# Pooled attention and an MLP mixer on one core: another first batch, single tails for batches 1 and 2, and an ungated load

## The chip, the cores and the metric

The kernel runs on one core of one Trainium2 chip. The metric is the device time of one execution in microseconds (us). The time before is 296.34 us, the median of 3 runs (295.75 to 296.78). The traces come from the hardware profiler; times in them count from the start of the profiled span.

## The reference, cut to what matters

There are 8 batches with 8 heads, 576 tokens and a head size of 64. Keys and values are averaged over 8 tokens, then attention and a mixer with token and channel mixing follow.

```python
k_p = k.reshape(B, H, Sp, pool, D).mean(axis=3)      # Sp = 72, pool = 8
v_p = v.reshape(B, H, Sp, pool, D).mean(axis=3)
scores = scale * np.matmul(q, k_p.transpose(0, 1, 3, 2))
attn = softmax(scores)                               # over the 72 pooled tokens
x = np.matmul(attn, v_p)                             # heads side by side: (B, 576, 512)
h = np.maximum(x.transpose(0, 2, 1) @ w_tok1, 0.0) @ w_tok2    # 576 -> 256 -> 576
u = x + h.transpose(0, 2, 1)
out = u + np.maximum(u @ w_ch1, 0.0) @ w_ch2         # 512 -> 1536 -> 512
```

## The kernel before

**Tiles.** The 576 tokens of a batch are 512 main tokens, as 128 rows of 4 (index j), and a tail of 64 tokens. Tails of two batches share a tile of 128 rows: `groups = [[0, 7], [1, 2], [3, 4], [5, 6]]`, `group_of` gives a batch's group and `slot_of` its half of the rows (`half[0]` is rows 0 to 63, `half[1]` rows 64 to 127). Tiles that the text names: `km`, `qm`, `vm` hold a batch's main tokens in bf16 (two buffers each), `kt`, `qt`, `vt` the tails, `kbd` the pooled keys, `vpx` the pooled values with a column of ones, `qT` the transposed queries, `prob_m` and `prob_t` the exponentials, `pT` these transposed, `x_main` and `x_tail` the attention's output, `u_main` the token mixing's, `uT_main` that transposed, `GT` the hidden layer of the channel mixing. `pa` (six buffers of one bank) and `pt` (two) are the PSUM tiles.

**Steps of a batch.** `pool_k` and `pool_v` average keys and values by matmuls with a pooling matrix (`pool_m`, and `pool_t` for the tails, whose rows outside the batch's half are zero). A `Unit` is half of the main tokens and a `TailUnit` a tail tile; their steps are `do_qT` (transposes of q), `do_S` (scores, maximum and difference on VectorE), `do_E` (exp on ScalarE), `do_PT` (transposes of the exponentials) and `do_AV` (values, by the helper `values`: matmuls, then a reciprocal and a product on VectorE). Then `token_mix`: `do_AT` or `do_both_AT` (first layer), `do_u` (second layer and residual) and `do_uT` (transposes). For batches 0 and 1 the transposes of q and the exponentials are matmuls; from batch 2 on they are DMAs on SyncE's queue, and so are those of u from batch 1 on. `channel_mix` gives blocks of the first channel layer (`do_GT`, four matmuls of 512 columns) and thirds of the second (`do_out`). `keep_running` issues matmuls on a tile of zeros, whose results nobody uses.

**Order.** The order on the engines is written by hand. `first_stream` is batch 0 up to its transposed u. Then for each batch b the channel mixing of b (`c_stream`) is woven with a side stream: `second_stream` (batch 1's attention and token mixing) and `score_stream(2)` for b = 0, later `value_stream(b + 1)` and `score_stream(b + 2)`. `weave` takes from both in proportion to planned costs; `delay` is the planned cost of main work ahead of the first side step. Each engine executes its own instructions in this order, and waits in front of one whose data are not there.

**Loads.** All loads are issued on GpSimd's queue (software DMA), in this order: batch 0, the token weights, `w_ch1`, `load(1)`, `w_ch2`, `load(2)`. These stand in the program ahead of the streams. `load(b)` brings a batch's three main tiles; the tails of both batches of a group come with the first of them, except for group 0. `load(3)` and later are issued by `load_gated`: a small copy on GpSimd that reads a tile of the running stream, so that the loads behind it start only then. For batch 3 the gate is the first values of batch 1.

Of the kernel before, what the change touches and what calls it, by code (L numbers as in the profile page):

```python
# [48 lines left out]
def kernel(  # L49
# [60 lines left out]
    for t in tail_t[0]:  # L110
        nc.vector.memset(t[half[1]], 0.0)

    def load(b):
        g = group_of[b]
        if g and slot_of[b] == 0:
            tail_t[g] = [tail_pool.tile([P, H, D], BF16, name=n) for n in ("kt", "qt", "vt")]
        main_t[b] = [kv_pool.tile([P, H, NJ, D], BF16, name=n) for n in ("km", "qm", "vm")]
        for i in (0, 2, 1) if slot_of[b] else (0, 1, 2):
            src, mt, tt = (k, q, v)[i], main_t[b][i], tail_t[g][i]
            nc.gpsimd.dma_start(out=mt.rearrange("p h j d -> p h (j d)"),  # L120
                                in_=src[b, :, 0:MAIN, :].rearrange("h (p j) d -> p h (j d)", j=NJ))

            for bb in [b] if g == 0 else groups[g] if slot_of[b] == 0 else []:
                nc.gpsimd.dma_start(out=tt[half[slot_of[bb]]], in_=src[bb, :, MAIN:S, :].rearrange("h p d -> p h d"))
# [58 lines left out]
    x_tail[0] = singles.tile([P, DM], BF16, name="xt0")  # L183
    nc.any.memset(x_tail[0][half[1]], 0.0)
# [47 lines left out]
    def pool_k(b):  # L232
        g, s = group_of[b], slot_of[b]
        km, kt = main_t[b][0], tail_t[g][0]
        kp_ps = ps.tile([P, HP, SP], FP32, name="pa")
        if b == 0:
            keep_running(kp_ps.rearrange("p r n -> p (r n)"), 18)
        for pr in range(HP):
            for j in range(NJ):
                for hl in range(2):  # L240
                    nc.tensor.matmul(out=kp_ps[hl * D:(hl + 1) * D, pr, 0:SPM], lhsT=km[:, 2 * pr + hl, j, :],  # L241
                                     rhs=pool_m[:, 0:SPM], start=(j == 0), stop=(j == NJ - 1))
        for pr in range(HP):
            for hl in range(2):
                nc.tensor.matmul(out=kp_ps[hl * D:(hl + 1) * D, pr, SPM:SP], lhsT=kt[:, 2 * pr + hl, :],
                                 rhs=pool_t[s][:, SPM:SP], start=True, stop=True)
        heads = kbd[b % NB].rearrange("p (r t) e n -> p r t e n", t=2)
        for hl in range(2):
            src = kp_ps[hl * D:(hl + 1) * D]
            nc.scalar.copy(out=heads[0:D, :, hl, 0, :], in_=src)  # L250
            nc.vector.tensor_copy(out=heads[D:P, :, hl, 1, :], in_=src)  # L251
# [10 lines left out]
    class Unit:  # L262
# [40 lines left out]
        def do_PT(self, e):  # L303
            self.pT[e] = pt_pool.tile([P, H, P], BF16, name="pT")
            if not self.by_pe:
                nc.sync.dma_start_transpose(out=self.pT[e], in_=self.probs[:, e].rearrange("p h n -> p (h n)"))
                return
            pT_ps = ps_tr.tile([SP, H, P], BF16, name="pt")
            for h in range(H):
                nc.tensor.transpose(out=pT_ps[:, h, :], in_=self.probs[:, e, h, 0:SP], identity=ident)  # L310
            (nc.scalar.copy if self.first else nc.vector.tensor_copy)(out=self.pT[e][0:SP], in_=pT_ps)  # L311

        def do_AV(self, e):
            values(self.pT[e], x_main[self.b][:, 2 * self.jj + e, :], slice(0, P), [(slice(0, P), self.b)],
                   2 if self.first else 0)

    def values(pT, xo, rows, pieces, extra, place=lambda h: h):
        w = rows.stop - rows.start
        for hf in range(2):
            ao = ps.tile([P, HP, D + 1], FP32, name="pa")  # L320
            keep_running(ao.rearrange("p h d -> p (h d)"), extra)
            for hh in range(HP):
                h = hf * HP + hh
                for r, b in pieces:
                    nc.tensor.matmul(out=ao[r, hh, :], lhsT=pT[0:SP, place(h), r], rhs=vpx[b % NB][:, h, :],  # L325
                                     start=True, stop=True)

            den = sm_pool.tile([P, HP], FP32, name="den")
            nc.vector.reciprocal(out=den[rows], in_=ao[rows, :, D])  # L329
            nc.vector.tensor_tensor(  # L330
                out=xo[rows, hf * HP * D:(hf + 1) * HP * D].rearrange("p (h d) -> p h d", d=D),
                in0=ao[rows, :, 0:D], in1=den[rows, :, None].broadcast_to([w, HP, D]), op=ALU.mult)

    class TailUnit:
# [19 lines left out]
        def do_S(self):  # L354
            w = self.rows
            sc = [ps.tile([P, HP, SP], FP32, name="pa") for _ in range(2)]
            for pr in range(HP):
                for hl in range(2):
                    for b in self.bs:
                        r = half[slot_of[b]]  # L360
                        nc.tensor.matmul(out=sc[hl][r, pr, :], lhsT=self.qT[hl * D:(hl + 1) * D, pr, r],
                                         rhs=kbd[b % NB][hl * D:(hl + 1) * D, 2 * pr + hl, hl, :],
                                         start=True, stop=True)
            self.sh = []
            for hl in range(2):
                mx = sm_pool.tile([P, 8], FP32, name="mx")
                nc.vector.tensor_reduce(out=mx[w, 0:HP], in_=sc[hl][w], axis=AX.X, op=ALU.max)
                sh = sh_pool.tile([P, 6, SP], FP32, name="sh")
                nc.vector.tensor_tensor(out=sh[w, 0:HP], in0=sc[hl][w],
                                        in1=mx[w, 0:HP, None].broadcast_to([w.stop - w.start, HP, SP]),  # L370
# [3 lines left out]
        def do_E(self):  # L374
            w = self.rows
            self.probs = prob_t[self.g % 2]
            for hl in range(2):
                nc.scalar.activation(out=self.probs[w, hl, :, 0:SP], in_=self.sh[hl][w, 0:HP], func=AF.Exp, scale=scale)

        def do_PT(self):  # L380
            w = self.rows
            self.pT = pt_pool.tile([P, H, P], BF16, name="pT")
            if not self.by_pe:
                nc.sync.dma_start_transpose(out=self.pT, in_=self.probs.rearrange("p e h n -> p (e h n)"))
                return
            pT_ps = ps_tr.tile([SP, H, P], BF16, name="pt")
            for h in range(H):
                nc.tensor.transpose(out=pT_ps[:, self.place(h), w], in_=self.probs[w, h % 2, h // 2, 0:SP],
                                    identity=ident[w, w])
            copy = nc.scalar.copy if self.first else nc.vector.tensor_copy  # L390
            copy(out=self.pT[0:SP, :, w], in_=pT_ps[:, :, w])

        @staticmethod
        def place(h):
            return (h % 2) * HP + h // 2

        def do_AV(self):
            values(self.pT, x_tail[self.g], self.rows, [(half[slot_of[b]], b) for b in self.bs],
                   2 if self.first else 0, self.place)

    def token_mix(b):
# [24 lines left out]
        def do_both_AT():  # L426
            at_ps = [ps.tile([P, DM], FP32, name="pa") for _ in range(2)]
            for m in range(2):
                mains(m, at_ps[m])
            for m in range(2):  # L430
                tails(m, at_ps[m])
            for m in range(2):
                acts(m, at_ps[m])
# [45 lines left out]
    def units(b):  # L479
# [4 lines left out]
        if g == 0:  # L484
# [6 lines left out]
        return parts[b]  # L491

# [3 lines left out]
    def mix_stream(st, b, pooled=()):  # L496
# [9 lines left out]
        if b == 0:  # L506
            add(2160, do_both_AT)
        else:
            add(1080, do_AT, 0)
            add(1080, do_AT, 1)  # L510
            for bb in pooled:
                add(KP, pool_k, bb)
# [7 lines left out]
    def first_stream():  # L520
# [4 lines left out]
        a, c, t = units(b)  # L525
        add(KP, pool_k, b)
        add(QT, a.do_qT, 0, HP)
# [4 lines left out]
        add(QT, c.do_qT, HP, H, copy=nc.vector.tensor_copy)  # L532
# [3 lines left out]
        add(0, c.do_E, 0)  # L536
        add(VP, pool_v, b)
        add(0, a.do_E, 1)
        add(SC, c.do_S, 1)
        add(0, a.do_E, 2)  # L540
        add(PT, a.do_PT, 0)
        add(SC, c.do_S, 2)
        add(PT, a.do_PT, 1)
        add(0, c.do_E, 1)
        add(QT, t.do_qT)
        add(AV, a.do_AV, 0)
        add(0, c.do_E, 2)
        add(SC, t.do_S)
        add(AV, a.do_AV, 1)
        add(PT, c.do_PT, 0)  # L550
        add(PT, c.do_PT, 1)
        add(AV, c.do_AV, 0)
        add(0, t.do_E)
        add(PT, t.do_PT)
        add(AV, c.do_AV, 1)
        add(AV, t.do_AV)
        mix_stream(st, b)
        return st

    def second_stream(st):  # L560
# [4 lines left out]
        add(KP, pool_k, b)  # L565
# [15 lines left out]
        add(0, load_gated, 3, lambda: x_main[1][:, 0, 0:1])  # L581
# [4 lines left out]
        add(KP, pool_k, 2)  # L586
        add(QT, t.do_qT)
        add(PT, c.do_PT, 0)
        add(2 * SC, t.do_S)
# [5 lines left out]
        add(VP, pool_v, 2)  # L595
        add(AV, t.do_AV)
        units(2)
        add(0, qT_dma, 2)
        mix_stream(st, b)

    def owned(b):

        g, s = group_of[b], slot_of[b]
        return [b] if g == 0 else groups[g] if s == 0 and g > 1 else []
# [56 lines left out]
    def channel_mix(uTs, us, dst, width):  # L661
# [37 lines left out]
        return [(864, do_GT(m0)) for m0 in range(0, NM, per)], out_pieces  # L699

    def c_stream(b):
# [11 lines left out]
        wide, chunk = channel_mix(uT_main[b], lambda j: u_main[b][:, j, :], dst_main, MAIN)  # L713
# [15 lines left out]
    load(2)  # L729
    engines = {mybir.EngineType.PE, mybir.EngineType.Activation, mybir.EngineType.DVE,  # L730
               mybir.EngineType.SP, mybir.EngineType.Pool}
    with tc.manual_schedule(engines=engines):
        weave(Stream(), first_stream())
        for b in range(B):
# [8 lines left out]
            weave(c_stream(b), side, 0.0 if b == 0 else 3456.0 if b == 1 else 1728.0, 3456.0 if b == B - 2 else 1728.0)  # L743
# [30 lines left out]
```

## Time and profile before

| | us |
|---|---|
| median of 3 runs | 296.34 |
| lowest, highest | 295.75, 296.78 |
| the profiled execution's own time | 295.11 |
| its span, first to last instruction | 293.4 |
| TensorE busy | 278.4 |
| VectorE, ScalarE, GpSimd busy | 166.3, 122.5, 49.3 |

The lines of the profile are read as follows. Engines are PE (matmul), PEld (weight load), DVE (VectorE), ACT (ScalarE), POOL (GpSimd) and SP (SyncE). A line of the timeline has the start and the length in us, the engine, the line of the kernel, the operation, output and inputs, and in brackets the idle time of the engine before it with what ended it. In the table of stages, a number in brackets is a count of instructions.

### The profile page before, as it was taken

How to read it: one execution, taken by the hardware profiler on the slowest of the kernel's cores; microseconds unless marked ns; L12 is line 12 of the kernel's file. 1: busy time of each engine (PE TensorE's matmuls, PEld its weight loads, DVE VectorE, ACT ScalarE, POOL GpSimd, SP SyncE). 2: the span in 40 equal slices, each digit the busy share in tenths (PEclk: the TensorE clock that was granted, in tenths of full speed). 3: DMA queues.
4: the chain of work that ended last, by engine and by line, in shares of the span. 5: the costliest groups of instructions: out<-in, count | busy, mean ns of one | idle time of the engine just before them, and what ended most of it. 6: DMA issues, size and time to landing. Idle time of an engine off the chain costs nothing.

```text
span 293.4 us, 5564 instructions
## 1 busy us (share of the span) xinstructions
PE 278.4 (95%) x2234; PEld 148.8 (51%) x2234; DVE 166.3 (57%) x382; ACT 122.5 (42%) x225; POOL 49.3 (17%) x80
## 2 busy tenths in 40 slices
PE   6778999998999999999999999999999999999994
PEld 3554555544545545456545444465445444464463
DVE  4776478868638944385558653684559642530012
ACT  7473667203652445125543445035433552026320
POOL 8656606300120008000300032000000000000000
PEclk9799999999999999999999999999999999999999
DMA  7999999996999999959998999759425920341013
GB/s 86 187 204 196 188 205 198 187 207 115 218 168 150 174 230 155 192 121 161 171 186 141 181 185 175 117 160 169 103 53 123 167 73 36 92 108 36 36 38 108
DMA packets 106843, 42.54 MB, mean 145 GB/s; under 512 B 73921, under 2 KB 102209, under 8 KB 106817
## 3 DMA queue, kind: packets, MB, share of 16 engines
q0 software_dynamic: 41392, 17.93, 49.2%
q1 hardware_dynamic: 65280, 24.13, 41.3%
q8 instruction: 17, 0.28, 0.4%
q10 hardware_dynamic: 144, 0.13, 0.1%
q14 instruction: 10, 0.07, 0.1%
HBM read 35.85 MB, written 9.44 MB: 154 GB/s over the span
## 4 chain that ended last, share of the span: by engine, by line
PE 81%; DMA 6%; ACT 5%; DVE 5%; POOL 2%; issue 1%; DVEq 0%; POOLq 0%
PE pa L673 30%; PE pa L688 28%; PE pa L414 4%; PE pa L442 4%; PE pa L325 3%; DMA vm<-in_v_dram 3%; PE pa L258 2%; DMA qT<-qm 2%; PE pa L286 2%; ACT pT L311 1%; DMA uTm<-um 1%; PE pa L450 1%; DVE mx L289 1%; PE pa L241 1%; DVE sh L291 1%; PE pa L418 1%
## 5 line engine op out<-in xcount | busy, mean ns | idle before, releaser
L688 PE MATMUL pa<-wc,GT 128*128 128x512 bf16 (+1 forms) x444 | 104.4, 373 | 0.0
L673 PE MATMUL pa<-uTm,wc 128*128 128x512 bf16 x384 | 92.9, 379 | 1.3 <-DMA uTm<-um 1.3
L675 ACT ACTIVATE GT<-pa 128x512 bf16<-128x512 f32 x108 | 64.5, 597 | 69.6 <-PE pa L673 69.5
L673 PEld LDWEIGHTS <-wc 128*128 128x128 bf16 x576 | 45.8, 98 | 38.4 <-DVE mx L289 1.7
L688 PEld LDWEIGHTS <-GT 128*128 128x128 bf16 x444 | 41.6, 98 | 40.5
L299 ACT ACTIVATE prob_m<-sh 128x432 bf16<-128x432 f32 (+1 forms) x48 | 24.4, 521 | 53.6 <-DVE sh L291 34.0
L692 DVE TENSOR_TENSOR o<-pa,um 128x512 f32<-128x512 f32 (+1 forms) x33 | 22.2, 672 | 31.0 <-PE pa L688 30.9
L289 DVE TENSOR_REDUCE mx<-pa 128x6 f32<-128x432 f32 (+1 forms) x48 | 26.4, 550 | 4.6 <-PE pa L286 4.5
L291 DVE TENSOR_TENSOR sh<-pa,mx 128x432 f32<-128x432 f32 (+1 forms) x48 | 26.8, 558 | 3.7
L330 DVE TENSOR_TENSOR xm<-pa,den 128x256 bf16<-128x256 f32 x64 | 27.2, 425 | 2.3
L329 DVE RECIPROCAL den<-pa 128x4 f32<-128x4 f32 (+1 forms) x74 | 13.0, 176 | 22.8 <-PE pa L325 22.8
L447 DVE TENSOR_TENSOR um<-pa,xm 128x512 bf16<-128x512 f32 x30 | 20.1, 687 | 5.5 <-PE pa L442 5.4
L325 PEld LDWEIGHTS <-pT 72*128 72x128 bf16 (+1 forms) x320 | 14.4, 100 | 9.3 <-issue 2.1
L442 PE MATMUL pa<-AT,w2m 128*128 128x512 bf16 x64 | 18.1, 379 | 0.5 <-ACT AT L408 0.5
L410 DVE TENSOR_SCALAR AT<-pa 128x512 bf16<-128x512 f32 x8 | 5.5, 692 | 22.2 <-PE pa L418 22.2
L658 POOL COPY gate<-pT 128x1 bf16<-128x1 bf16 x4 | 0.8, 188 | 102.6 <-DMA pT<-prob_m 102.6
L286 PE MATMUL pa<-kbd,qT 128*128 128x144 bf16 x128 | 16.3, 234 | 1.0 <-DMA qT<-qm 0.5
L325 PE MATMUL pa<-vpx,pT 72*128 72x65 bf16 (+1 forms) x320 | 16.6, 194 | 0.4 <-ACT pT L311 0.4
L286 PEld LDWEIGHTS <-qT 128*128 128x128 bf16 x128 | 11.2, 101 | 10.8 <-ACT qT L277 1.2
L414 PE MATMUL pa<-xm,w1m 128*128 128x512 bf16 x64 | 16.3, 379 | 0.0
L251 DVE CAST kbd<-pa 64x288 bf16<-64x288 f32 x16 | 7.3, 456 | 12.1 <-ACT kbd L250 12.0
L230 PE MATMUL pa<-idle 128*128 128x288 bf16 (+2 forms) x44 | 10.8, 366 | 2.2 <-DVE pool_t L159 2.2
(99 smaller groups left out, 211.5 us busy)
## 6 DMA issues: line engine op xcount, KB each, us to landing
out_dram<-o SPq DMA_DIRECT2D x31, 256.0 KB, 2.5
km<-in_k_dram POOLq DMA_DIRECT2D x8, 512.0 KB, 7.8
vm<-in_v_dram POOLq DMA_DIRECT2D x8, 512.0 KB, 10.6
qm<-in_q_dram POOLq DMA_DIRECT2D x7, 512.0 KB, 10.0
wc<-in_moe_w_ch_dram POOLq DMA_DIRECT2D x6, 512.0 KB, 10.7
out_dram<-o SPq DMA_DIRECT2D x9, 128.0 KB, 2.4
kt<-in_k_dram POOLq DMA_DIRECT2D x8, 64.0 KB, 6.5
qm<-in_q_dram POOLq DMA_DIRECT2D x2, 256.0 KB, 5.1
```

Of the source, the lines that this page charges most:

```text
L286: nc.tensor.matmul(out=sc[:, (h - h0) * 2:(h - h0) * 2 + 2, :], lhsT=qTs[self.b][:, 2 * h + self.jj, :], rhs=kbd[self.b % NB][:, h], start ...
L289: nc.vector.tensor_reduce(out=mx[:, 0:n], in_=sc, axis=AX.X, op=ALU.max)
L291: nc.vector.tensor_tensor(out=sh[:, 0:n], in0=sc, in1=mx[:, 0:n, None].broadcast_to([P, n, SP]), op=ALU.subtract)
L299: nc.scalar.activation(out=self.probs[:, :, h0:h1, 0:SP].rearrange("p e h n -> p h e n"), in_=self.sh[i][:, 0:(h1 - h0) * 2].rearrange("p ...
L325: nc.tensor.matmul(out=ao[r, hh, :], lhsT=pT[0:SP, place(h), r], rhs=vpx[b % NB][:, h, :], start=True, stop=True)
L330: nc.vector.tensor_tensor(out=xo[rows, hf * HP * D:(hf + 1) * HP * D].rearrange("p (h d) -> p h d", d=D), in0=ao[rows, :, 0:D], in1=den[ro ...
L414: nc.tensor.matmul(out=at_ps, lhsT=w1m[:, j, m * P:(m + 1) * P], rhs=x_main[b][:, j, :], start=(j == 0), stop=False)
L442: nc.tensor.matmul(out=u_ps, lhsT=w2m[:, m, j, :], rhs=ATs[b][:, m, :], start=(m == 0 and not by_act), stop=(m == 1))
L673: nc.tensor.matmul(out=g_ps[:, i, :], lhsT=wc1[:, kk, m * P:(m + 1) * P], rhs=uTs[:, kk, :], start=(kk == 0), stop=(kk == 3))
L675: nc.scalar.activation(out=GT[:, m0:m0 + per, :], in_=g_ps, func=AF.Relu)
L688: nc.tensor.matmul(out=hold["ps"], lhsT=GT[:, kk, j * P:(j + 1) * P], rhs=wc2[:, kk, cols], start=(kk == 0), stop=(kk == NM - 1))
L692: nc.vector.tensor_tensor(out=o_sb, in0=hold["ps"], in1=us(j)[:, cols], op=ALU.add)
```

## The change

- Batch 0: the pooled keys of even and odd heads go to two PSUM banks, ScalarE copies the one and VectorE the other. Idle matmuls: 28 instead of 18 ahead of `pool_k`, 6 of 512 columns behind it (`warm`), and one instead of two for each half in `values`, where sums and values of all 8 heads now have one bank each and one reciprocal and one product. The tail's steps come earlier, the first token layer (`do_both_AT`) is in three pieces among the last values, and `pool_k` of batch 1 stands among the transposes of batch 0's u, its copies behind them.
- The first three blocks of batch 0's channel mixing are done in halves of 256 tokens (`do_early`), and its side stream starts behind a planned cost of 3456 instead of 0.
- A `TailUnit` of a single batch puts even and odd heads on the two halves of the rows of one bank, so that it has one maximum, one difference and one exp, and four transposes instead of eight. The tails of batches 1 and 2 are units of their own now: batch 1's is transposed by matmuls, batch 2's by DMAs. They still share the tiles `kt1`, `qt1`, `vt1`, which are no longer part of a pool; each batch loads its own half, and their other half is cleared first.
- `pool_k(2)` and `pool_v(2)` leave the second stream for batch 1's token mixing and batch 2's score stream.
- `load(3)` is called ahead of the streams, with no gate.

The diff, cut to its core:

```diff
+    tail_t[1] = [singles.tile([P, H, D], BF16, name=n) for n in ("kt1", "qt1", "vt1")]
     def load(b):
-        if g and slot_of[b] == 0:
+        if g > 1 and slot_of[b] == 0:
             tail_t[g] = [tail_pool.tile([P, H, D], BF16, name=n) for n in ("kt", "qt", "vt")]
...
-            for bb in [b] if g == 0 else groups[g] if slot_of[b] == 0 else []:
+            for bb in [b] if g < 2 else groups[g] if slot_of[b] == 0 else []:
                 nc.gpsimd.dma_start(out=tt[half[slot_of[bb]]], in_=src[bb, :, MAIN:S, :].rearrange("h p d -> p h d"))
...
+    for t in tail_t[1]:
+        nc.any.memset(t[half[1]], 0.0)
...
     def pool_k(b):
+        pool_k_copy(b, pool_k_sum(b))
+
+    def pool_k_sum(b):
         km, kt = main_t[b][0], tail_t[g][0]
-        kp_ps = ps.tile([P, HP, SP], FP32, name="pa")
+        kp_ps = [ps.tile([P, HP, SP], FP32, name="pa") for _ in range(2)]
         if b == 0:
-            keep_running(kp_ps.rearrange("p r n -> p (r n)"), 18)
+            keep_running(kp_ps[0].rearrange("p r n -> p (r n)"), 28)
...
-                nc.tensor.matmul(out=kp_ps[hl * D:(hl + 1) * D, pr, SPM:SP], lhsT=kt[:, 2 * pr + hl, :],
+                nc.tensor.matmul(out=kp_ps[hl][hl * D:(hl + 1) * D, pr, SPM:SP], lhsT=kt[:, 2 * pr + hl, :],
                                  rhs=pool_t[s][:, SPM:SP], start=True, stop=True)
+        return kp_ps
+
+    def pool_k_copy(b, kp_ps):
         for hl in range(2):
-            src = kp_ps[hl * D:(hl + 1) * D]
-            nc.scalar.copy(out=heads[0:D, :, hl, 0, :], in_=src)
-            nc.vector.tensor_copy(out=heads[D:P, :, hl, 1, :], in_=src)
+            src = kp_ps[hl][hl * D:(hl + 1) * D]
+            copy = nc.vector.tensor_copy if hl else nc.scalar.copy
+            copy(out=heads[0:D, :, hl, 0, :], in_=src)
+            copy(out=heads[D:P, :, hl, 1, :], in_=src)
...
     class TailUnit:
         def do_S(self):
-            sc = [ps.tile([P, HP, SP], FP32, name="pa") for _ in range(2)]
+            sc = [ps.tile([P, HP, SP], FP32, name="pa") for _ in range(len(self.bs))]
...
+                        dst = sc[hl][r, pr, :] if len(sc) > 1 else sc[0][half[hl], pr, :]
...
     def first_stream():
         add(KP, pool_k, b)
+        add(0, warm, 6)
...
-        mix_stream(st, b)
+        add(1080, do_both_AT, (0, 1), False, False)
         add(AV, c.do_AV, 0)
         add(AV, c.do_AV, 1)
+        add(1080, do_both_AT, (2,), True, False)
+        add(540, do_both_AT, (3,), False, True)
+        for j in range(NJ):
+            add(690, do_u, j)
+        add(224, do_uT, 0)
+        add(224, do_uT, 1)
+        k1 = []
+        add(KP, lambda: k1.append(pool_k_sum(1)))
+        add(224, do_uT, 2)
+        add(224, do_uT, 3)
+        add(0, lambda: pool_k_copy(1, k1[0]))
...
     def second_stream(st):
-        add(KP, pool_k, b)
...
-        add(0, load_gated, 3, lambda: x_main[1][:, 0, 0:1])
...
-        add(KP, pool_k, 2)
...
-        add(2 * SC, t.do_S)
+        add(SC, t.do_S)
...
-        add(VP, pool_v, 2)
-        add(AV, t.do_AV)
         units(2)
         add(0, qT_dma, 2)
-        mix_stream(st, b)
+        add(AV, t.do_AV)
+        mix_stream(st, b, owned(2))
...
     load(2)
+    load(3)
...
-            weave(c_stream(b), side, 0.0 if b == 0 else 3456.0 if b == 1 else 1728.0, 3456.0 if b == B - 2 else 1728.0)
+            weave(c_stream(b), side, 3456.0 if b <= 1 else 1728.0, 3456.0 if b == B - 2 else 1728.0)
```

## The prediction

> **Bounds now.** I read the busy times first, then the busy time of each engine by stage, then the timeline around the stages that the change touches, then GpSimd's own queue of loads with the time from issue to landing.
>
> ```profile
> PE 278.4 (95%) x2234; PEld 148.8 (51%) x2234; DVE 166.3 (57%) x382; ACT 122.5 (42%) x225; POOL 49.3 (17%) x80
> ```
>
> TensorE is busy for 278.4 of 293.4 us. Where the other 15 us lie is told by the stages (columns: stretch, its length, busy PE, PEld, DVE, ACT, POOL, granted clock, DMA, GB/s):
>
> ```profile
> 30.00:35.00 5.00, 4.50 (x74) 2.85 (x74) 2.19 (x5) 3.02 (x6) 3.59 (x5) 1.00 1.75 183
> 65.00:70.00 5.00, 4.49 (x33) 2.44 (x32) 4.12 (x8) 1.46 (x3) 0.00 (x0) 1.00 0.83 137
> 100.00:150.00 50.00, 50.00 (x384) 26.22 (x383) 28.01 (x68) 21.63 (x39) 9.76 (x14) 1.00 1.08 172
> 200.00:250.00 50.00, 50.00 (x347) 24.64 (x346) 27.20 (x67) 21.26 (x39) 0.00 (x0) 1.00 0.48 100
> ```
>
> From 100 to 250 us TensorE has no gap at all. So there is no slack to the right in which a late start could be caught up: what delays TensorE in the first 80 us delays the end by as much, and what it is given there is given to the end.
>
> Three places of the timeline fix the pace of that first part:
>
> ```profile
> 32.96 0.69 PE L241 MATMUL pa<-pool_m,km 128*64 128x64 bf16 x32
> 33.71 1.02 PE L673 MATMUL pa<-uTm,wc 128*128 128x512 bf16 x4
> 65.91 0.55 PE L286 MATMUL pa<-kbd,qT 128*128 128x144 bf16 x6 [0.51 <-DMA qT<-qm]
> 72.67 3.61 PE L673 MATMUL pa<-uTm,wc 128*128 128x512 bf16 x16 [1.27 <-DMA uTm<-um]
> ```
>
> At 32.96 the keys of batch 1 are pooled, at 33.71 the channel mixing of batch 0 begins, at 72.67 that of batch 1. The brackets are the only waits for a DMA between them: 0.51 and 1.27 us.
>
> The loads are a queue of their own:
>
> ```profile
> 20.10 0.88 POOL L120 DMA_DIRECT2D km<-in_k_dram  x1
> 20.98 1.38 POOL L124 DMA_DIRECT2D kt<-in_k_dram  x2
> 33.24 0.90 POOL L120 DMA_DIRECT2D km<-in_k_dram  x1
> 46.50 0.19 POOL L658 COPY gate<-xm 128x1 bf16<-128x1 bf16 x1 [9.57 <-DVE xm L330]
> 46.99 0.88 POOL L120 DMA_DIRECT2D km<-in_k_dram  x1 [0.30 <-PE pa L325]
> ```
>
> They land strictly in the order of issue, one behind the other. By the times to landing of single issues, batch 1's k lands at 20.10 + 8.7 = 28.8, its first k tail at 20.98 + 8.2 = 29.2, its last v tail at 29.05 + 7.6 = 36.6, the three pieces of w_ch2 at 29.72 + 9.5 = 39.2, 30.47 + 11.2 = 41.7 and 32.51 + 11.7 = 44.2. Batch 2's k, issued at 33.24, lands last of these:
>
> ```profile
> L120 POOL DMA_DIRECT2D km<-in_k_dram x1: 903/903/903, 33.2 to 33.2; - x1
> DMA to landing us min/median/max: 13.9/13.9/13.9
> ```
>
> So at 47.1 us. A 512 KB load takes 2.5 to 2.9 us of this queue and a tail 0.4 us, and it has no gap from the first landing on.
>
> **The wait.** The change adds one wait that decides the result. Before, the tails of batches 1 and 2 are both loaded by load(1), in one tile of 128 rows, and both halves are there at 29.6 when pool_k(1) runs at 32.96. After, load(1) brings rows 0 to 63 alone, and load(2) brings rows 64 to 127 of the same tile, kt1. But pool_k(1) still takes `kt[:, 2 * pr + hl, :]`, all 128 rows (the rows of the other batch meet zeros in pool_t). load(2) stands ahead of all streams in the program, so the tail matmuls of pool_k(1) must wait for a DMA of batch 2. The order of the changed program with its waits agrees: the first tail weight load of pool_k(1) waits for two DMA semaphores, one of batch 1's k tail and one that counts up to batch 2's k tail. That DMA now stands behind k, q and v of batch 1, all of w_ch2 and batch 2's k.
>
> When does it land? Between the landing of batch 1's k (28.8) and of batch 2's k (47.1) the queue loses three tails, 3 x 0.43 = 1.3 us, and batch 2's k tail adds 0.4: 47.1 - 1.3 + 0.4 = 46.2 us. GpSimd issues about eight loads ahead, as before, so the queue stays fed.
>
> Queued on TensorE behind the waiting weight load: the last two transposes of u of batch 0, the channel mixing of batch 0 and all that follows. ScalarE and VectorE wait for these in their turn. After 46.2 come the 8 tail matmuls (0.12) and the two transposes (2 x 0.22): the first block of channel mixing starts at 46.2 + 0.1 + 0.12 + 0.45 = 46.9. Before: 33.71. That is a delay of 13.2 us.
>
> **Its cover.** All edits of the first batch end before this wait. Two banks for the pooled k and one engine for each make four copies in a row (8.11 to 9.91, 1.8 us) two pairs side by side (0.9). Ten more idle matmuls end near 7.9 instead of 6.7, past k's landing at 7.2 (+0.6), and six of 512 columns cost 1.3 ahead of the q transposes. The tail halves its passes on VectorE (four of 0.45 become two), its two exps of 0.39 become one of some 0.43, one pT copy (0.96) leaves ScalarE, and of the first token mixing's ten matmuls (2.15 us, 25.98 to 28.1) only two follow the last values. Walking that order by these rows, TensorE comes to the waiting weight load near 30 to 31 instead of 33.5. All this is costed at nothing, because the wait ends at 46.2 whether TensorE came at 30 or at 36. Without that cover it would be worth about 3 us, as the first rival has it. The early half-width blocks of channel mixing are the same columns in pieces, 24 x 0.11 for 12 x 0.22, nothing. The ungated load(3) is worth nothing: before, its gate opened at 46.50 while load(2) filled the queue until 52.4, so the queue never ran dry. Now its q and v wait for batch 1's transposes and pool_v (52 to 55) and land by some 62; batch 3's scores come 30 us later.
>
> **The clock.** TensorE will stand still for some 15 us. What the trace shows of this:
>
> ```profile
> 2.17 4.50 PE L230 MATMUL pa<-idle 128*128 128x288 bf16 x18 [2.17 <-DVE pool_t L159]
> 11.00:12.00 1.00, 1.00 (x12) 1.00 (x10) 0.96 (x3) 0.17 (x1) 0.56 (x1) 0.50 1.39 184
> 12.00:13.00 1.00, 1.00 (x9) 0.60 (x7) 0.97 (x2) 0.87 (x2) 0.00 (x0) 0.50 1.71 177
> ```
>
> After the idle start, 18 matmuls took 0.24 us each, twice the pace of later ones, for 4.3 us. Between 5 and 10 us TensorE was busy for 3.3 of 5, and the granted clock then was 0.5 for 3.4 us (0.58, 0.50, 0.50, 0.71 in four stretches of 1 us). So after the long wait I expect half speed for 3.4 to 4.3 us, which loses half of that, 1.7 to 2.15. I take 1.9. Bounds: nothing if the clock were kept, 3.4 if half speed lasted twice as long. The Trainium skill (TensorE: Matmul & The Clock Gate, "What's actually happening") says that the clock falls to half after an idle window of about 3.4 us and comes back after one busy window of that length, wherever that window happens to begin. An estimate by that page alone would be 1.7 us, and the sum 0.2 us lower.
>
> **Next stage.** From there to the channel mixing of batch 1 it took 72.67 - 33.71 = 39.0 us before. The waits of 0.51 and 1.27 us for DMA transposes go, since the loads are done by 62 and these transposes come after 70: -1.8. The tail of batch 1 now has nothing between its transposes and its values. Before, pool_v(2) (1.1 us) and a block of 0.86 stood there, while VectorE worked off four value pairs and then copied pT, until 56.6, with the transposes done at 55.6. That is a new wait of 1.0. Two tails of 8 score and 8 value matmuls (0.32 and 0.26 each) instead of one of 16 (0.32 and 0.38) add 0.4, less 4 transposes that move to the DMA queue (0.2). Sum -1.8 + 1.0 + 0.2 = -0.6, between -1.8 (the new wait hidden) and +1.2 (the old ones stay). pool_k(2) moves behind batch 1's first token mixing, its k there since 46: nothing. Later stages keep their order; batch 7's tail loses two VectorE passes in a stage bound by TensorE: nothing.
>
> **Sum.** 13.2 + 1.9 - 0.6 = +14.5 us. The profiled execution took 295.11 us (span 293.4): 309.6. The median of the runs is 296.34, 1.2 above it: 310.8 us.
>
> **Rivals.** (1) Faster: the wait for batch 2's k tail does not hold TensorE, the two halves being kept apart. Then the first batch's gain of 3 us comes through up to 58 us, but there the scores of batch 2 wait for its q transposes, which landed at 65.9 before, 1.8 us after the last load (55.31 + 8.8 = 64.1). They may be issued near 52 now, yet the loads still end at 63 to 64, and a transposing DMA issued at 150.7 under loads landed 6.1 us later, where the median is 2.5. The end gains between 0 and 3, say 2: 294.3. It decides the other way if the tail matmuls start by 34. For it: the rows that pool_k(1) uses are there at 29.2. Against: it reads the whole tile, and the wait is in the order. Chance 0.03. The Trainium skill (DMA: Bandwidth & Descriptors, "Queues, rings and completion order") says that each DMA engine takes its queues in turn, packet by packet; by that these transposes would land under the loads, and this rival would keep the full 3 us, 293.3. (2) The clock stays full, or the wait is all that happens: 310.8 - 1.9 = 308.9. Against it stand the two stretches at half speed. Chance 0.10. (3) Half speed lasts twice as long and the new tail wait does not replace the old ones: +1.5 and +1.8, 314.1. Chance 0.05.
>
> **Numbers.** The forecast has 0.82. A measurement of this kernel tells about 0.3% (0.9 us) from no change; only the first rival comes near or below it. Faster 0.03, same 0.01, slower 0.96. The range takes in rival (2) less 0.9 us for the landing and the stage, and the forecast plus 2.2 us for a longer half-speed stretch: 308.0 to 313.0.
>
> **Signs.** Right: one TensorE gap of 15 to 16 us, ended by a DMA into kt at 45.5 to 47; granted clock 0.5 right behind it for 3 to 5 us; the first block of channel mixing at 46.5 to 48; batch 1's at 86 to 88; no gap from 100 to 250 us. Wrong: pool_k(1) goes through before 34 us, or the gap ends at another transfer, or TensorE comes back at full clock.

## The result and the profile after

The changed kernel takes 309.84 us, the median of 4 runs (309.58 to 310.35), for 296.04 us of the kernel before (the three runs above and a fourth, 294.78 to 296.78). The ratio is 1.0473, with a 95% interval of 1.0433 to 1.0513: slower. The forecast was 310.8 us. Below, each ratio is to runs of the kernel before that were made beside the run in question; their medians lie between 295.33 and 295.64 us. One run of all (301.08 us, in experiment 6) lies more than 1.5% above the fastest of its kernel and is left out of its ratio. The profiled execution took 309.79 us with a span of 308.1; before it was 295.11 with 293.4.

First the busy times of the profile's page:

```profile
PE 280.5 (91%) x2279; PEld 151.6 (49%) x2279; DVE 163.5 (53%) x372; ACT 123.5 (40%) x227; POOL 49.1 (16%) x79
```

TensorE has 2.1 us more of busy time than before, and some 12.6 us more of idle time. One gap alone is longer than that. The timeline of the changed kernel (start us, us, engine, line, operation, out<-in, count, and in brackets the idle time before it and what ended it):

```profile
30.00 0.69 PE L248 MATMUL pa<-pool_m,km 128*64 128x64 bf16 x32
46.24 0.38 PE L252 MATMUL pa<-pool_t,kt 128*64 128x8 bf16 x8 [15.55 <-DMA kt<-in_k_dram]
46.55 1.03 PE L502 MATMUL pt<-ident,um 128*128 128x128 bf16 x8
47.38 4.03 PE L756 MATMUL pa<-uTm,wc 128*128 128x256 bf16 x24
```

L248 is the main part of pool_k(1), L252 its tail part. The tail comes 15.55 us behind the main part, released by a transfer into kt, and the first block of channel mixing (L756) stands at 47.38, where it was 33.71. The issue of that transfer, and who waited for it:

```profile
L125 POOL DMA_DIRECT2D kt<-in_k_dram x1: 687/687/687, 32.5 to 32.5; - x1
...
  PEld L252: 15.7, 1
  PE pa L252: 15.5, 1
...
DMA to landing us min/median/max: 13.7/13.7/13.7
```

32.48 + 13.72 = 46.20: it is load(2)'s k tail, and its only customer is the tail of pool_k(1). The stages, with the same columns as before:

```profile
35.00:40.00 5.00, 0.00 (x0) 0.00 (x0) 0.00 (x0) 0.00 (x0) 2.26 (x3) 0.50 1.25 206
47.00:48.00 1.00, 1.00 (x9) 0.83 (x7) 0.77 (x2) 0.38 (x1) 0.42 (x1) 0.50 1.77 183
49.00:50.00 1.00, 1.00 (x7) 0.69 (x6) 0.00 (x0) 0.00 (x0) 0.88 (x2) 0.54 1.48 196
50.00:51.00 1.00, 1.00 (x11) 0.90 (x10) 0.00 (x0) 0.43 (x1) 0.48 (x1) 1.00 1.78 180
100.00:150.00 50.00, 49.69 (x410) 26.29 (x405) 33.13 (x70) 18.30 (x35) 6.94 (x10) 1.00 1.05 168
```

In the gap the granted clock falls to 0.50, and it comes back only at 49.9 us, 3.7 us after the matmuls start again. From 100 us on TensorE has no gap to speak of, as before.

Batch 1's channel mixing begins at 87.27 (72.67 before), 14.6 us later, and the span ends 14.7 us later. So the whole loss is made before 88 us and nothing of it comes back.

### The profile page after: what moved, and what is told of

Same layout as the page of the kernel before. It is cut to its first block, busy times and chain, and to the rows that moved or that the text cites. A ratio compares the mean times of both kernels' runs of the same rounds, so it can differ in the third digit from the quotient of the medians.

```text
span 308.1 us, 5672 instructions
## 1 busy us (share of the span) xinstructions
PE 280.5 (91%) x2279; PEld 151.6 (49%) x2279; DVE 163.5 (53%) x372; ACT 123.5 (40%) x227; POOL 49.1 (16%) x79
## 4 chain that ended last, share of the span: by engine, by line
PE 77%; DMA 12%; DVE 4%; POOL 4%; ACT 1%; issue 1%; DVEq 0%; POOLq 0%
PE pa L725 30%; PE pa L740 27%; DMA kt<-in_k_dram 4%; PE pa L444 4%; PE pa L482 3%; DMA qm<-in_q_dram 3%; DMA w2r<-in_moe_w_tok_dram 3%; PE pa L358 3%; PE pa L269 2%; PE pa L297 2%; DMA uTm<-um 1%; PE pa L756 1%; PE pa L248 1%; PE pa L448 1%; PE pa L490 1%; DVE um L487 1%
## 5 line engine op out<-in xcount | busy, mean ns | idle before, releaser
L727 ACT ACTIVATE GT<-pa 128x512 bf16<-128x512 f32 x105 | 62.6, 597 | 68.3 <-PE pa L725 68.2
L725 PE MATMUL pa<-uTm,wc 128*128 128x512 bf16 x372 | 89.8, 379 | 0.0
L725 PEld LDWEIGHTS <-wc 128*128 128x128 bf16 x564 | 45.0, 98 | 35.8 <-issue 0.2
L363 DVE TENSOR_TENSOR xm<-pa,den 128x256 bf16<-128x256 f32 x56 | 23.8, 425 | 1.9
L362 DVE RECIPROCAL den<-pa 128x4 f32<-128x4 f32 (+1 forms) x66 | 11.7, 177 | 21.9 <-PE pa L358 21.9
L358 PEld LDWEIGHTS <-pT 72*128 72x128 bf16 (+1 forms) x280 | 12.5, 100 | 8.9 <-issue 1.7
L252 PE MATMUL pa<-pool_t,kt 128*64 128x8 bf16 x64 | 2.3, 176 | 15.5 <-DMA kt<-in_k_dram 15.5
L358 PE MATMUL pa<-vpx,pT 72*128 72x65 bf16 (+1 forms) x280 | 14.1, 194 | 1.1 <-DVE pT L422 1.0
L444 PE MATMUL pa<-xm,w1m 128*128 128x512 bf16 x56 | 14.4, 379 | 0.0
```

What stands on the lines that cost most here:

```text
L358: nc.tensor.matmul(out=ao[r, hh, :], lhsT=probs_of(h, r), rhs=vpx[b % NB][:, h, :], start=True, stop=True)
L363: nc.vector.tensor_tensor(out=xo[rows, hf * HP * D:(hf + 1) * HP * D].rearrange("p (h d) -> p h d", d=D), in0=ao[rows, :, 0:D], in1=den[ro ...
L444: nc.tensor.matmul(out=at_ps, lhsT=w1m[:, j, m * P:(m + 1) * P], rhs=x_main[b][:, j, :], start=(j == 0), stop=False)
L725: nc.tensor.matmul(out=g_ps[:, i, :], lhsT=wc1[:, kk, m * P:(m + 1) * P], rhs=uTs[:, kk, :], start=(kk == 0), stop=(kk == 3))
L727: nc.scalar.activation(out=GT[:, m0:m0 + per, :], in_=g_ps, func=AF.Relu)
```

## Experiments

The theory: one shared tile makes batch 1's pooled keys wait for batch 2's k tail; the landing of that tail sets the time. Rivals: other edits of the change make the delay; the clock's loss is not real; and, once the wait is gone, something else holds the same time. What was expected is quoted as it was put down before each run.

### 1. Read only the batch's own rows

```diff
-lhsT=kt[:, 2 * pr + hl, :],  rhs=pool_t[s][:, SPM:SP]
+lhsT=kt[half[s], 2 * pr + hl, :],  rhs=pool_t[s][half[s], SPM:SP]
-lhsT=pool_t[s], rhs=vt
+lhsT=pool_t[s][half[s]], rhs=vt[half[s]]
```

> The changed kernel, except that the tail matmuls of pool_k and pool_v read only the 64 rows of their own batch (64 partitions of kt1 and pool_t for 128). Loads, order and everything else stay. Theory (one shared tile makes batch 1's pooled keys wait for batch 2's k tail): TensorE passes this place at 30.2 us, as the k tail of batch 1 landed at 29.3; the first block of channel mixing starts near 31 (46.9 was the forecast, 33.71 the kernel before); the whole delay goes and the first batch's gain of 2.8 us comes through: 292 to 294 us, the likeliest 293. Rival A (the delay is mainly from other edits: first batch's order, single tails, ungated fourth batch's loads): the time stays above 296. Rival B (the wait is only moved: the next shared tile, or the transposes of batch 2's q under the loads, holds TensorE instead): a wait of several us between 35 and 65, and 297 to 309.

Measured: 296.63 us (10 runs, 296.05 to 298.03), ratio to before 1.0046 (1.0024 to 1.0067). Its timeline:

```profile
30.26 0.69 PE L248 MATMUL pa<-pool_m,km 128*64 128x64 bf16 x32
30.88 0.29 PE L252 MATMUL pa<-pool_t,kt 64*64 64x8 bf16 x8
...
63.91 0.55 PE L297 MATMUL pa<-kbd,qT 128*128 128x144 bf16 x6 [1.37 <-DMA qT<-qm]
```

The tail follows the main part at once. With the same loads in the same order, 13.2 of the 13.8 us are gone: the wait makes them, and rival A falls as their cause, though 296.63 lies above the 296 that it named. The forecast of 293 was missed by 3.6 us. Rival B has a part in that: TensorE waits 1.37 us for batch 2's transposed q, and batch 1's channel mixing starts at 72.54, hardly earlier than before (72.67). Another 1.7 us are lost behind it, where no such wait shows (span 295.0 for 293.4). Experiments 5 to 9 take these apart.

### 2. The kernel before with one part of the change

```diff
-for bb in [b] if g == 0 else groups[g] if slot_of[b] == 0 else []:
+for bb in [b] if g < 2 else groups[g] if slot_of[b] == 0 else []:
```

> The kernel before, with one part of the change alone: load(1) brings only batch 1's tails, load(2) batch 2's, in the same shared tiles. First batch's order, the double tail and the gated fourth batch stay as before. Theory: its pool_k(1) waits for batch 2's k tail, which lands at 46.2; the first block of channel mixing starts at 46.4 for 33.71, +12.7; half speed behind it costs another 1.8; the waits of 0.5 and 1.3 us for transposes may go: 307.8 to 309.6 us. Rival A (other edits make the delay): within 1 us of 295 to 296.

Measured: 309.35 us (one run, span 307.6).

```profile
45.87 0.38 PE L245 MATMUL pa<-pool_t,kt 128*64 128x8 bf16 x8 [11.20 <-DMA kt<-in_k_dram]
```

One line of the load is enough to make the whole loss. TensorE came to it some 4 us later than in the changed kernel, so the gap is 11.20 for 15.55 us, and the time is the same within 0.5 us: this is the cover that the prediction claimed for the first batch's edits. The two are not alike term by term: here the first block stands at 46.18 for 47.38, and half speed lasts until 51.5 for 49.9.

### 3. A dose: the same tails earlier in the queue

```diff
 # in load_w_ch2, behind the first of its three pieces:
+if i == 0:
+    for src, tt in ((k, tail_t[1][0]), (v, tail_t[1][2])):
+        nc.gpsimd.dma_start(out=tt[half[1]], in_=src[2, :, MAIN:S, :]...)
 # and load(2) leaves these two out
```

> The changed kernel, with batch 2's k and v tails moved ahead in the queue of loads, behind the first third of w_ch2 and no longer behind batch 2's k and v. Reads of all 128 rows stay. Theory: batch 2's k tail lands 7.8 us earlier (38.4 for 46.2, behind one third of w_ch2 at 38.0); the wait of TensorE ends there and shrinks from 15.5 to 7.8 us; the time falls by the same 7.8 us to 302.0; half speed behind it, as the stand is still longer than 3.4 us, costs 1.8 as before. If the clock's loss went with the length of the stand, 301.1. Rival A: no change, 309.8.

Measured: 301.98 us (one run, span 300.3).

```profile
38.19 0.38 PE L255 MATMUL pa<-pool_t,kt 128*64 128x8 bf16 x8 [7.03 <-DMA kt<-in_k_dram]
```

The wait ends 8.05 us earlier and the time is 7.9 us lower. The landing sets the time one for one, and a stand of 7 us costs the clock about as much as one of 15: the stage rows of this run show half speed until 42.3, 4.2 us behind the stand, for 3.7 in the changed kernel. The variant in which the loss goes with the length of the stand (301.1) is out by 0.9.

### 4. TensorE kept busy while it waits

```diff
+if b == 1:
+    keep_running(ps.tile([P, DM], FP32, name="pa"), 68)   # ahead of the tail matmuls
```

> The changed kernel with 68 idle matmuls of 512 columns (14.5 us at full clock) ahead of the waiting tail matmuls of pool_k(1), into a PSUM buffer of their own. Theory: they fill 30.4 to 45 of the stand; the wait still ends at 46.2; TensorE keeps full clock behind it and the 1.8 us at half speed go: 308.0 us. Rival (the clock would stay high anyway or its loss is hidden by the following stage): 309.8. If idle matmuls run at half clock, they take 29 us and the time rises to about 324.

Measured: 307.71 us (4 runs, 307.60 to 307.93), 2.1 us below the changed kernel; ratio to before 1.0420 (1.0389 to 1.0450). The timeline and one stage:

```profile
30.77 14.85 PE L234 MATMUL pa<-idle 128*128 128x512 bf16 x66
45.92 0.29 PE L254 MATMUL pa<-pool_t,kt 128*64 128x8 bf16 x8 [0.29 <-DMA kt<-in_k_dram]
```

```profile
47.00:48.00 1.00, 1.00 (x11) 0.90 (x10) 0.92 (x3) 0.99 (x3) 0.10 (x1) 1.00 1.66 187
```

The wait still ends at 45.9, the clock is 1.00 behind it, and 2.1 us come back, of which 0.3 are an earlier landing (45.92 for 46.24). So the clock's part is about 1.8 us. It reaches the end: batch 1's channel mixing starts at 85.24 for 87.27, and the span is 306.1 for 308.1.

### 5. Both tails in load(1) again

```diff
-for bb in [b] if g < 2 else groups[g] if slot_of[b] == 0 else []:
+for bb in [b] if g == 0 else groups[g] if slot_of[b] == 0 else []:
```

> The changed kernel with one part undone: load(1) brings both tails of batches 1 and 2 again, as the kernel before does. All reads are of 128 rows; first batch's order, single tails and ungated load(3) stay. Theory: the 15.5 us wait goes as in the run with 64-row reads; the transposes of batch 2's q, issued near 52 under the fourth batch's loads, land near 64 as there and hold TensorE until then, so of the first batch's 2.8 us little is left at batch 1's channel mixing (72.3 for 72.67); but the 0.11 us per pool_k and 0.21 us per pool_v that 64-row reads cost in that run are gone, 1.6 us of them behind 72 us: 294.7 to 295.7 us, level with the kernel before. Rival (64-row reads are free and the other 1.6 us of that run come from single tails): 296.6. Rival 2 (transposes don't hold the end): 292.5 to 293.

Measured: 295.30 us (10 runs, 294.62 to 297.28), ratio 1.0003 (0.9976 to 1.0030): level with the kernel before, as forecast.

```profile
30.57 0.27 PE L252 MATMUL pa<-pool_t,kt 128*64 128x8 bf16 x8
30.78 0.62 PE L502 MATMUL pt<-ident,um 128*128 128x128 bf16 x8
31.23 2.02 PE L756 MATMUL pa<-uTm,wc 128*128 128x256 bf16 x17
...
64.05 0.55 PE L297 MATMUL pa<-kbd,qT 128*128 128x144 bf16 x6 [2.17 <-DMA qT<-qm]
65.95 0.32 PE L395 MATMUL pa<-kbd,qTt 64*64 64x72 bf16 x8 [0.36 <-DMA qTt<-qt]
```

The channel mixing starts at 31.23 for 33.71, so the first batch's edits do gain 2.5 us there. At 64.05 the gain meets batch 2's transposed q and 2.5 us of waits eat most of it: batch 1's channel mixing starts at 72.10 for 72.67. The transposing DMA itself:

```profile
DMA to landing us min/median/max: 12.1/12.1/12.1
```

Issued at 51.89, it landed at 64.00, in the middle of the fourth batch's loads (61.88 the one before it, 66.05 the one behind).

### 6. The fourth batch's q and v behind these transposes

```diff
 # load(b, which) brings the named ones of k, q, v (0, 1, 2)
-load(3)
+load(3, (0,))            # k alone
 ...
 add(0, qT_dma, 2)
+add(0, load_gated, 3, lambda: qTs[2][:, 0, 0:1], (1, 2), False)   # q and v
```

> The kernel of the previous run, but load(3) brings k alone at once; its q and v wait until the transposed q of batch 2 has landed. Theory (the loads of the fourth batch, queued without a gate, hold up the transposes): the transposes, issued near 52, land at 57 to 59 for 64; the wait of 1.4 us before batch 2's scores goes; the loads of q and v move to 62 to 69, where batch 1's u is transposed, which lands at 69 to 71; batch 1's channel mixing starts at 70 to 71 for 72.3: 1.3 to 2.3 us less than the previous run, 293 to 294. Rival (the transposes are slow by themselves or from the first half of loads): no change beyond 0.5 us. Rival 2 (u's transposes are held in turn): no change, with a wait for uTm of 1 to 2 us.

Measured: 298.84 us (10 runs, 296.19 to 301.08), ratio 1.0090 (1.0057 to 1.0123): 3.5 us slower than run 5. Two lines of it, the landing of the transposed q and TensorE's wait:

```profile
DMA to landing us min/median/max: 5.4/5.4/5.4
```

```profile
75.80 5.27 PE L727 MATMUL pa<-uTm,wc 128*128 128x512 bf16 x16 [5.68 <-DMA uTm<-um]
```

The mechanism holds: transposed q lands in 5.4 us for 12.1, and no wait is left before batch 2's scores. But the forecast of 293 to 294 was missed by some 5 us: the loads now meet the transposes of batch 1's u, whose last piece lands at 75.66. That is the second rival, and its price was put far too low (5.68 us for 1 to 2, with half speed behind it: 16 matmuls in 5.27 us for 3.61 before).

### 7 and 9. Staged loads, with and without the copy on ScalarE

```diff
 add(0, qT_dma, 2)
+add(0, load_gated, 3, lambda: qTs[2][:, 0, 0:1], (1,), False)     # q
 ...
+add(0, load_gated, 3, lambda: c.pT[1][:, 0, 0:1], (2,), False)    # v, at the head of load(4)
+add(0, load, 4)
 # run 7 alone:
-copy = nc.scalar.copy if self.first else nc.vector.tensor_copy    # the tail's pT
+copy = nc.scalar.copy
```

> As the previous run, but v of load(3) waits further, at the head of load(4), and the tail's pT copy of batch 1 is on ScalarE instead of VectorE. Theory: the wait of 1.0 us for that copy, which was put down to VectorE's four value pairs ahead of it, goes; only q loads while u of batch 1 is transposed; batch 1's channel mixing starts at 69 to 70, another 1 us earlier: 292 to 293. Rival (later loads of batches 3 and 4 come late in their turn): waits for a DMA between 85 and 105 and no gain over the previous run.

> The kernel with staged loads (k of load(3) at once, q behind batch 2's transposes, v at the head of load(4)), but the tail's pT copy of batch 1 back on VectorE. It parts the two edits of that run. Theory (the loads alone make the gain over the kernel before; the copy only shortens a wait from 1.03 to 0.67 us, while the start of that run lost 0.47 at another place): within 0.5 us of 292.7. Rival (the copy was worth its 1.0 us): 293.7.

Measured: 292.67 us with the copy (4 runs, 292.55 to 292.80; ratio 0.9891, 0.9849 to 0.9934) and 292.73 us without it (5 runs, 292.33 to 293.88; ratio 0.9917, 0.9877 to 0.9958). Both beat the kernel before, whose medians beside them were 295.64 and 295.33 us, by 3.0 and 2.6 us. The timeline of the run without the copy:

```profile
61.79 0.54 PE L298 MATMUL pa<-kbd,qT 128*128 128x144 bf16 x6
...
69.95 3.62 PE L730 MATMUL pa<-uTm,wc 128*128 128x512 bf16 x16
```

Neither the scores of batch 2 nor batch 1's channel mixing waits for a DMA, and the latter starts 2.7 us earlier than before (72.67). The gain reaches the end once both transposes are free of loads. Not all of it need be the first batch's: the kernel before also waited for these two transposes (0.51 and 1.27 us), and no run staged the loads there alone. In run 7 the wait for the tail's pT fell only to 0.67 us. The wait of 0.47 us that the expectation of run 9 puts down to run 7 alone (at 27.9, for AT) stands in the changed kernel and in run 9 too, so it does not set run 7 apart. The copy is worth nothing that these runs can tell.

### 8. 64-row reads alone

The edit of run 1, put into the kernel before.

> The kernel before, and only the tail matmuls of pool_k and pool_v read 64 rows for 128. No load and no wait is touched. Theory (TensorE loses about 0.1 us on each passage between 128-row and 64-row operands): 8 pool_k at 0.11 and 8 pool_v at 0.21 make 2.6 us, of which up to 0.9 before 66 us lies in front of two waits for DMA transposes and is hidden: 1.6 to 2.6 us slower than before, 297.2 to 298.2. Rival (64-row reads are free): 295.5.

Measured: 297.23 us (10 runs, 296.79 to 298.85), ratio 1.0052 (1.0030 to 1.0073): 1.6 us slower, at the lower end of what was expected. One pool_v of before, then the same one of this run:

```profile
99.99 1.03 PE L258 MATMUL pa<-vm,pool_m 128*72 128x512 bf16 x4
100.85 0.38 PE L259 MATMUL pa<-vt,pool_t 128*72 128x512 bf16 x1
101.06 1.03 PE L688 MATMUL pa<-wc,GT 128*128 128x512 bf16 x4
```

```profile
100.16 1.03 PE L258 MATMUL pa<-vm,pool_m 128*72 128x512 bf16 x4
101.11 0.40 PE L259 MATMUL pa<-vt,pool_t 64*72 64x512 bf16 x1
101.45 1.04 PE L688 MATMUL pa<-wc,GT 128*128 128x512 bf16 x3
```

From the first start to that of the channel mixing it takes 1.07 us before and 1.29 here, though the tail matmul has the same 512 columns: 0.09 us more ahead of it and 0.13 behind it. The Trainium skill (TensorEngine Tiling (Array Packing), "Key Properties") says that a change of tiling mode drains TensorE, and gives no time for it. These rows fit that, with about 0.1 us for each passage between 128 and 64 rows; that a drain is what takes this time, no row shows.

### 10. The fourth batch gated again

```diff
 # run 5, and:
-load(3)
+add(0, load_gated, 3, lambda: x_main[1][:, 0, 0:1])   # behind a.do_AV(0) of batch 1
```

> The kernel with both tails in load(1), and the fourth batch's loads gated again as in the kernel before (its gate opens near 45.6, when batch 1's first values are there). Theory (the gate does not matter, as the queue is full until 52 either way and all of load(3) still lies in front of the transposes): batch 2's transposed q lands near 64 as without the gate, and the time is 295.3 within 0.5 us. Rival (the missing gate lets the loads crowd the transposes): the transposes land 2 us earlier or more and the time is 293.5 to 294.5.

Measured: 296.85 us (10 runs, 295.39 to 299.48), ratio 1.0059 (1.0021 to 1.0098). The forecast of 295.3 within 0.5 was missed by 1.0 us. The interval overlaps that of run 5, and the runs spread over 4 us. In the profiled one the transposed q landed at 65.19 (64.00 in run 5), so the gate did not free the transposes, and the rival falls. The wait for it:

```profile
65.24 0.90 PE L297 MATMUL pa<-kbd,qT 128*128 128x144 bf16 x6 [3.00 <-DMA qT<-qm]
```

It is 3.00 us for 2.17 in run 5, and behind it the granted clock is 0.50 until 68.6 (1.00 all the way in run 5): the six matmuls take 0.90 us for 0.55. Half of these 3.4 us and the 1.2 us of the later landing, less the second wait of run 5 (0.36, not here), come to 2.5; the two profiled executions (296.92 and 294.62) are 2.3 us apart. The two executions of this run with a mean granted clock of 1.00 took 295.39 and 295.50 us, level with run 5. What the gate itself costs stays open.

## Why the prediction was right

**The wait.** Place, cause and end were as put: the weight load of pool_k(1)'s tail, the transfer into kt, landing forecast at 46.2 and seen at 46.20. Runs 1, 2 and 5 show the cause from three sides: reads kept apart, the part alone, the part undone. Run 3 shows the size.

**First block, 46.9 forecast, 47.38 seen.** The missing 0.5 us is half speed: the tail matmuls and the two transposes were counted at full clock, and the whole clock term was put behind the first block. The sum had it once, under the clock, so it came out right.

**Its cover.** Right as far as this kernel goes: run 2 has the old first batch and the same time. Of the 3 us named for the case without cover, 2.2 and 2.5 showed at the channel mixing of runs 1 and 5 (31.56 and 31.23 for 33.71). A gain reached the end only where the loads were staged (runs 7 and 9), and how much of it is theirs no run tells.

**The clock, 1.9 forecast.** Half speed lasted from 46.24 to 49.9: 3.7 us, of which half is lost, 1.8. Run 4 gives 1.8 by taking it away. The second rival (308.9, full clock) falls with it. So does the third (314.1): half speed lasted no 7 us, and the two old waits went.

**Next stage, -0.6 forecast.** From the first block to batch 1's channel mixing it took 87.27 - 47.38 = 39.9 us, for 39.0 before. Of the +0.9, 1.3 us are the rest of the half speed ((49.9 - 47.38) / 2), so the stage itself gave -0.3 to -0.4. The two old waits did go, and the new one for the tail's pT was 1.03 us for 1.0. Its reason, VectorE's work ahead of the copy, is shown only in part: with the copy on ScalarE (run 7) 0.67 us stayed.

```profile
70.55 0.44 PE L358 MATMUL pa<-vpx,pT 72*64 72x65 bf16 x8 [1.03 <-DVE pT L422]
```

Two small waits that the sum didn't have (0.34 at 64.87, 0.29 at 83.51) more than make up the difference of 0.3; the rest was not taken apart. One sentence of this step was wrong: the transposes of batch 2's q don't come after 70 but at 52.04, under the fourth batch's loads, and landed at 59.36 and 63.69. It cost nothing here, as their scores come at 80: the -1.8 came true, but half of its reason was luck. With the wait gone these transposes cost 2.5 us (run 5).

**Ungated load(3), nothing.** Not refuted in this kernel: it is under the same cover. Its q and v landed by 65.8, not 62, with those transposes under way beside them.

**The sum.** 309.6 was forecast for a profiled execution and 309.79 seen. The median forecast is 1.0 high because 1.2 us were added for the distance of the profiled execution from the median; here that distance is 0.05. This is the only term that missed by as much as 1 us.

**The first rival's price.** 294.3 was given for the wait gone, a gain of 2 us; run 5 took 295.30 us, 0.3 less than the kernel before beside it. What failed in it is the 6.1 us taken for a transposing DMA under loads: with the whole of load(3) in the queue it took 12.1 (7.3 in the changed kernel, where q of load(3) was issued only behind it, at 54.33). The prediction had weighed a rule of the Trainium skill (DMA: Bandwidth & Descriptors, "Queues, rings and completion order") that each DMA engine takes its queues in turn, by which the full 3 us would be kept. Loads and transposes did move side by side (beside them a q load of run 1 took 3.4 us, between the landings at 55.55 and 58.98, for 2.6 alone), yet the transposes were late.

**The signs.** One gap of 15.55 us ended at 46.24 by a DMA into kt, half speed for 3.7 us behind it, first block at 47.38, batch 1's at 87.27, 0.3 us of idle time from 100 to 250 us: all as named.

**Left open.** What the single tails and the early half-width blocks are worth by themselves was not tried; runs 1, 5, 6, 7, 9 and 10 hold both beside the first batch's order. Nor was the staging of runs 7 and 9 tried on the kernel before.

## What to carry to other kernels

A dependency goes by what an instruction reads, not by what it needs: when a load is split, look for every reader of the tile that still takes all of its rows, and cost the wait at the landing of the last half, behind all that stands ahead of it in the queue. An edit that is ready early is worth nothing until the next transfer that it meets is early too, so follow a gain from stage to stage to the end before adding it. A long stand of TensorE costs more than its own length; an idle matmul stream that ends with the wait takes that extra back.

## What the runs showed of the hardware

- Half speed came in whole pieces of about 3.41 us. In the stage rows at 1 us or finer it lasted from 32.9 to 49.9 in the changed kernel, from 37.9 to 51.5 in run 2 and from 35.5 to 42.3 in run 3: 17.1, 13.7 and 6.8 us, five, four and two pieces. So how long it lasts behind a stand depends on where the stand ends in a piece: 3.7 us, 5.7 us and 4.2 us. The Trainium skill (TensorE: Matmul & The Clock Gate, "What's actually happening") has windows of that length, and these rows agree. But a whole piece without work is not needed: in the changed kernel half speed began 2.2 us after the last matmul, so a piece that ended there held some 1.2 us of work. In run 10 a stand of 3.00 us was followed by one piece at half speed (65.2 to 68.6); in run 5 one of 2.17 us was not.
- A transposing DMA of 512 KB took 12.1 us to land with all of the next batch's loads queued (run 5) and 5.4 us with one load and its two tails left (run 6). Keeping q and v of those loads out of its way, and v out of the way of the next transposes, was worth 2.6 us (295.30 in run 5, 292.73 in run 9).
- A matmul over 64 rows between matmuls over 128 costs about 0.1 us on each side (run 8), and halving the rows of the tail matmuls of pool_k and pool_v made the kernel 1.6 us slower.
